# Attention, Fourier mixing and a feed-forward block in one kernel: the queries cut into seven tiles of 64 instead of four tiles of 64 and four of 49

## The chip, the cores and the metric

One Trainium2 chip, one of its cores. The time is the device time of one execution in microseconds (us). The kernel before took 907.45 us in the median of three runs (907.34 to 907.94). The profiled execution took 908.43 us, of which 906.0 us lie between its first and last instruction (its span), and 2.4 us around them.

## The reference

```python
def _attn_ref(q, k, v, cap):                      # q, k, v: 4 x 12 x 448 x 64, float32
    scores = (1 / np.sqrt(64)) * np.matmul(q, k.transpose(0, 1, 3, 2))
    scores = cap * np.tanh(scores / cap)
    scores = scores - np.max(scores, axis=-1, keepdims=True)
    attn = np.exp(scores)
    attn = attn / (np.sum(attn, axis=-1, keepdims=True) + 1e-09)
    return np.matmul(attn, v)

def _moe_ref(x, w_ch1, w_ch2):                    # x: 4 x 448 x 768, the 12 heads side by side
    mixed = np.real(np.fft.fft(np.fft.fft(x, axis=1), axis=2))
    u = x + mixed
    un = (u - mean(u)) / np.sqrt(var(u) + 1e-06)  # over the 768 features
    ch = np.maximum(un @ w_ch1, 0.0) @ w_ch2      # 768 x 3072, 3072 x 768
    return u + ch
```

## The kernel before, in words

Four batches; in each, twelve heads are worked on as six pairs, so 24 pairs follow each other. Keys lie on the partitions. `scores` (line 410) multiplies 64 keys of each of two heads (or 128 of one) with all queries: four products of 64 x 64 weights side by side in the four quarters of TensorE's array, 450 columns each, into one of two PSUM tiles `s`. ScalarE makes `tanh` (line 420) and `exp` (line 423) of each tile of 900 columns into one of five tiles `a`. `weigh` (line 439) takes 64 queries of `a` as weights and streams the values `vt` through them: 64 value columns and one column of ones, from which the denominators come. One pair of heads has seven units of `weigh`; six have 128 keys of one head, the seventh (the first unit of odd pairs, the last of even ones) has 64 keys of both. All of a pair adds up in one PSUM tile `av`, of which there is only one.

The queries are reordered into four groups of 112, 113, 112 and 113 rows (`ROWS`; the queries 0 and 224 stand twice, 450 in all), so that the four groups lie over each other: group 2 holds the mirror images of group 0, group 3 those of group 1, and the Fourier transform over the sequence begins with sums and differences of groups (`fold_tokens`). `weigh` cuts each group into 64 and 49 queries (where a group has 112, the last is the next group's first): four times two products for a unit of one head, the two of a pair side by side in the two column halves of the array, with the same values streamed through both.

When a pair is complete, VectorE adds the guard to the denominators (line 454), takes their reciprocals (455) and multiplies the whole tile with them into `u` (461, one instruction of 512 columns on 113 partitions). Only then is `av` free for the first product of the next pair. When the six pairs of a batch are there, VectorE folds them (480 to 500), TensorE makes two Fourier stages (`yps`, line 516; `pq`, line 544), VectorE combines and adds (536, 564, 568), takes moments and standardises, TensorE transposes (`pt`, line 628), and VectorE and ScalarE split the result into a high and a low part (`xs`). This work of a batch runs while the pairs of the next batch are in attention. VectorE also splits the weights of the feed-forward block into high and low parts (lines 675 to 709).

The feed-forward block is 3,450 products of 128 x 448 (`ph`, line 762; `po`, lines 797 and 820), twelve groups of four batches. The first group is interleaved with the last batch's Fourier work.

All instructions stand in one written plan: a table `ORDER` gives each step a number, the plan is sorted by it, and every engine executes its instructions in this order. DMAs are issued by SyncE in the same order, apart from the first load of queries.

Of the kernel before, what the change touches and what calls it, by code (L numbers as in the profile page):

```python
# [34 lines left out]
KODD, KEVEN = list(range(1, H2 // 2, 2)), list(range(0, H2 // 2 + 1, 2))  # L35
# [7 lines left out]
CNT = [len(r) for r in ROWS]  # L43
OFF = [sum(CNT[:g]) for g in range(4)]
R = max(CNT)

NT2 = CNT[0] + CNT[1] + 1

PERM = ROWS[0] + ROWS[1] + ROWS[2] + ROWS[3][2:]
OUT = [sum(CNT[:g]) for g in range(4)]  # L50

# [5 lines left out]
NK = len(KODD + KEVEN)  # L57
# [44 lines left out]
        265, 256, 308, 286, 489, 482, 521, 495, 721, 724, 710, 712, 839, 840, 844, 846  # L102
    ],
    "combine": [
        230, 249, 234, 245, 431, 437, 450, 453, 663, 673, 655, 684, 830, 832, 831, 833
    ],
    "denominators": [
        44, 74, 103, 125, 155, 178, 205, 246, 282, 317, 343, 372, 417, 464, 500, 537, 561, 596, 649,
        678, 715, 750, 776, 801
    ],  # L110
    "exp": [
# [19 lines left out]
    "load_constant": [
        214, 212, 237, 22
    ],
    "load_k": [
        0, 4, 6, 40, 43, 113, 134, 147, 186, 195, 257, 264, 344, 306, 389, 433, 456, 516, 519, 570, 583,
        672, 707, 719
    ],
    "load_q": [
        1, 12, 3, 34, 20, 61, 99, 108, 101, 144, 143, 169, 207, 232, 220, 262, 295, 302, 321, 342, 363,
        392, 427, 425, 462, 504, 492, 528, 543, 572, 619, 646, 657, 727, 726, 737  # L140
    ],
    "load_v": [
# [39 lines left out]
    "rows_copy": [
        362, 574, 794, 874
    ],
    "rows_out": [
        381, 444, 505, 466, 606, 622, 623, 615, 802, 814, 871, 824, 875, 900, 887, 877
    ],
    "scales": [
        2
    ],  # L190
    "scores": [
# [5 lines left out]
    ],  # L197
    "stage1": [
        224, 236, 226, 241, 419, 424, 438, 448, 647, 664, 644, 677, 827, 826, 829, 821
    ],  # L200
    "stage2": [
        260, 253, 293, 273, 469, 468, 490, 485, 717, 718, 691, 701, 837, 838, 843, 845
    ],
    "standardise": [
        348, 365, 357, 364, 575, 564, 550, 592, 780, 792, 782, 783, 883, 881, 867, 876
    ],
    "tanh": [
# [5 lines left out]
    ],  # L213
    "u_cols": [
        371, 374, 384, 391, 404, 407, 593, 594, 604, 607, 634, 636, 797, 798, 811, 812, 853, 860, 884,
        885, 889, 890, 892, 897
    ],
    "u_copy": [
        373, 376, 388, 395, 408, 420, 597, 599, 616, 618, 635, 642, 800, 805, 816, 823, 855, 865, 886,
        888, 893, 896, 898, 899  # L220
    ],
    "warmup": [
        8
    ],
    "weigh": [
# [54 lines left out]
def attention_fft_ffn(  # L280
# [60 lines left out]


    vt = new([P, 2, NC, D + 1], F32, "vt", 1, "vt")
    nc.gpsimd.memset(vt[:, :, :, D:], 1.0)

    qk = {}

# [109 lines left out]
    def normalise(p):  # L457
# [5 lines left out]
            pa[..., :D],  # L463
            den.to_broadcast([R, 4, 2, D]),
            op=mul,
        )

# [581 lines left out]
```

## Time and profile before

| | us |
|---|---|
| median of three runs | 907.45 |
| the profiled execution | 908.43 |
| its span | 906.0 |
| PE busy (TensorE's products) | 896.0 |
| DVE busy (VectorE) | 713.5 |
| ACT busy (ScalarE) | 326.6 |
| POOL busy (GpSimd) | 6.8 |

The granted TensorE clock is 1.00 of full speed throughout. PE counts products, whose ends are modelled, so 99% busy does not mean that it could do nothing more. ScalarE is busy 70% and more only in the first eight of 40 slices, which is the attention; VectorE is at 80% or more in most slices from the fourth on. Three stretches are of use: from 0 to 55 us the first batch is in attention alone; from 55 to 192.6 us the other pairs are in attention beside the Fourier work of the batches before; from 192.6 to about 268.5 us the last batch's Fourier work goes on beside the first products; after that the feed-forward block runs alone.

### The profile page before, as it was taken

To read this page: it belongs to the slowest core of one execution; us is meant where nothing else is said; L and a number is where in the kernel's file an instruction comes from. 1 tells how busy PE (TensorE), PEld (TensorE's weight loads), DVE (VectorE), ACT (ScalarE), POOL (GpSimd) and SP (SyncE) were. 2 spreads that over 40 slices of the span, in tenths; PEclk is the share of its full clock that TensorE was granted. 3 is DMA by queue.
4 is the path that set the end of the run, shared out by engine and by line. 5 is a ranking of instruction groups with operands and counts; after the bars stand their busy time and mean duration, and the time that the engine had idled before them with its cause. 6 is when DMAs were issued, how large, how long until landed. Compare 5 with 4: busy or idle time off the path is not lost.

```text
span 906.0 us, 18642 instructions
## 1 busy us (share of the span) xinstructions
PE 896.0 (99%) x7836; PEld 791.7 (87%) x7836; DVE 713.5 (79%) x1444; ACT 326.6 (36%) x503; POOL 6.8 (1%) x15
## 2 busy tenths in 40 slices
PE   9999999999899999999999999999999999999998
PEld 5667777788889999999999999999999999999998
DVE  3578889989998788888878788787787877878633
ACT  7988999962412222122122221212222122122200
POOL 0000000000000000000000000000000000000000
PEclk9999999999999999999999999999999999999999
DMA  6545444300202221211222111112211112121033
GB/s 203 163 141 137 112 119 129 108 8 1 91 18 74 60 71 52 63 53 53 68 60 68 54 52 53 53 54 66 57 53 54 53 53 57 57 62 53 18 122 122
DMA packets 50467, 66.64 MB, mean 74 GB/s; under 512 B 25424, under 2 KB 36560, under 8 KB 50384
## 3 DMA queue, kind: packets, MB, share of 16 engines
q1 hardware_dynamic: 50096, 65.13, 24.9%
q8 instruction: 61, 1.00, 0.4%
q10 hardware_dynamic: 288, 0.33, 0.1%
q14 instruction: 22, 0.18, 0.1%
HBM read 59.93 MB, written 5.52 MB: 72 GB/s over the span
## 4 chain that ended last, share of the span: by engine, by line
PE 94%; DVE 3%; ACT 1%; issue 0%; DMA 0%; SPq 0%; POOL 0%; DVEq 0%; POOLq 0%
PE ph L762 37%; PE po L797 37%; PE av L439 8%; PE s L410 7%; PE pq L544 2%; PE yps L516 1%; PE pt L628 1%; DMA vt<-vr 0%; PE warm L351 0%; DVE xs L329 0%; DVE xc L752 0%; DVE y L536 0%; ACT a L420 0%; DVE xc L829 0%; DVE hh L774 0%
## 5 line engine op out<-in xcount | busy, mean ns | idle before, releaser
L762 PE MATMUL ph<-xs,w 128*128 128x448 f32 x1728 | 352.8, 362 | 0.0
L797 PE MATMUL po<-hh,w 128*128 128x448 f32 (+1 forms) x1686 | 343.5, 362 | 3.2 <-DVE xc L829 3.2
L762 PEld LDWEIGHTS ph<-xs,w 128*128 128x128 f32 x1728 | 323.6, 187 | 21.8
L797 PEld LDWEIGHTS po<-hh,w 128*128 128x128 f32 x1686 | 314.4, 188 | 26.4 <-DVE xc L829 4.4
L805 DVE TENSOR_TENSOR xc<-xc,po 128x448 f32<-128x448 f32 (+1 forms) x281 | 172.3, 617 | 41.1 <-PE po L797 40.8
L675 ACT ACTIVATE wt<-raw 128x384 f32<-128x384 f32 x84 | 46.7, 555 | 229.0 <-DVE w L709 229.0
L774 DVE SCALAR_TENSOR_TENSOR hh<-ph,hh 128x448 fp32r<-128x448 f32 x96 | 60.0, 625 | 86.4 <-ACT hh L773 85.7
L773 ACT ACTIVATE hh<-ph 128x448 fp32r<-128x448 f32 x96 | 52.4, 545 | 177.3 <-PE ph L762 177.3
L439 PEld LDWEIGHTS av<-vt,a 128*49 128x49 f32 (+3 forms) x3072 | 85.3, 130 | 23.6 <-issue 12.6
L439 PE MATMUL av<-vt,a 128*49 128x65 f32 (+3 forms) x3072 | 91.2, 222 | 1.4 <-issue 0.9
L420 ACT ACTIVATE a<-s,tscale 128x900 f32<-128x900 f32 x84 | 82.7, 1017 | 10.2 <-PE s L410 9.9
L324 ACT CAST w<-wt 128x384 fp32r<-128x384 f32 x84 | 42.8, 510 | 119.1 <-DVE wt L684 119.1
L423 ACT ACTIVATE a<-a,capt 128x900 f32<-128x900 f32 x84 | 84.8, 1051 | 0.5
L410 PE MATMUL s<-q,k 64*64 64x450 f32 x672 | 75.7, 555 | 0.5 <-ACT a L420 0.4
L684 DVE SCALAR_TENSOR_TENSOR wt<-wt 128x384 f32<-128x384 f32 x96 | 53.6, 558 | 9.2
L681 DVE SCALAR_TENSOR_TENSOR wt<-raw,wt 128x384 uint32<-128x384 uint32 x96 | 53.6, 559 | 3.3
L709 DVE TENSOR_TENSOR w<-wt 128x384 fp32r<-128x384 f32 x96 | 53.6, 558 | 3.3
L703 DVE SCALAR_TENSOR_TENSOR wt<-raw,wt 128x384 f32<-128x384 uint32 x96 | 53.5, 558 | 2.9
L329 DVE TENSOR_TENSOR wt<-wt,w 128x384 f32<-128x384 f32 x96 | 52.8, 550 | 0.0
L410 PEld LDWEIGHTS s<-q,k 64*64 64x64 f32 x672 | 21.4, 134 | 23.0 <-issue 10.3
L678 DVE TENSOR_SCALAR wt<-raw 128x384 uint32<-128x384 uint32 x96 | 34.2, 357 | 1.1
L700 DVE TENSOR_SCALAR wt<-wt 128x384 uint32<-128x384 uint32 x96 | 34.0, 354 | 0.5
(63 smaller groups left out, 345.2 us busy)
## 6 DMA issues: line engine op xcount, KB each, us to landing
raw<-w2r SPq DMA_DIRECT2D x48, 384.0 KB
raw<-w1r SPq DMA_DIRECT2D x48, 384.0 KB
q<-qr SPq DMA_DIRECT2D x35, 225.5 KB
outT<-xc SPq DMA_DIRECT2D x23, 224.0 KB
k<-kr SPq DMA_DIRECT2D x12, 256.0 KB
vt<-vr SPq DMA_DIRECT2D x24, 128.0 KB
k<-kr SPq DMA_DIRECT2D x12, 192.0 KB
vt<-vr SPq DMA_DIRECT2D x24, 96.0 KB
```

Of the source, the lines that this page charges most:

```text
L410: nc.tensor.matmul(ps_t[t][h * D : (h + 1) * D, n, :SQ], kt[q, k][rows, k0, h], qk[q, x][rows, :SQ], start=True, stop=True,)
L420: nc.scalar.activation(a_t[t], ps_t.pop(t)[:, :, :SQ], AF.Tanh, scale=tscale)
L423: nc.scalar.activation(a_t[t], a_t[t], AF.Exp, scale=capt)
L439: nc.tensor.matmul(pa_t[p][q0:q1, j, g * (D + 1) : (g + 1) * (D + 1)], a_t[t][rows, n, OFF[g] + q0 : OFF[g] + q1], vt[rows, p % 2, i], sta ...
L681: nc.vector.scalar_tensor_tensor(tu, hi.bitcast(U32), 0xC0000000, tu, op0=ALU.bitwise_and, op1=ALU.bitwise_or)
L684: nc.vector.scalar_tensor_tensor(t, w, HI_MIN, t, op0=ALU.is_ge, op1=mul)
L703: nc.vector.scalar_tensor_tensor(w, lo, 2.0**-52, w, op0=mul, op1=mul)
L709: nc.vector.tensor_tensor(ws[c][1][:, sl], t, w, op=add)
L762: nc.tensor.matmul(ph[:, :S], w_[:, dc * P : (dc + 1) * P], x_, start=(k_ == 0), stop=(k_ == 3 * NDC - 1),)
L774: nc.vector.scalar_tensor_tensor(hh[:, 1], ph[:, :S], 0.0, f32(hh[:, 0]), op0=ALU.max, op1=sub)
L797: nc.tensor.matmul(po[:, q0:q1], w_[:, dc * P : (dc + 1) * P], hh[:, x_, q0:q1], start=(k_ == 0), stop=(k_ == 3 * GF - 1),)
L805: nc.vector.tensor_tensor(ac[:, q0:q1], ac[:, q0:q1], po[:, q0:q1], op=add)
```

## The change

The queries 0 and 224 no longer stand twice: 448 queries, seven tiles of 64. The rows now lie in four groups of 128, 128, 96 and 96. The first 96 of groups 0 and 1 have their mirror images in groups 2 and 3; the last 32 of groups 0 and 1 are queries of which both mirror halves are kept unfolded.

In `weigh`, a unit of one head has six products (three times two column halves) instead of eight. The seventh tile of a head is issued together with that of the other head of the pair: one goes to the lower column half, the other to the upper, in the unit of the second head, each with its own values streamed through. For the unit of both heads it is twelve products and then the two seventh tiles, one in a lower and one in an upper quarter. So a pair has 56 products instead of 64. The ones now stand in front of the values, and two products of a pair write 66 columns instead of 65.

`normalise` has five VectorE instructions instead of one: a product of 128 columns on 32 partitions, a memset of two columns, two products of 64 columns on 64 partitions, and one of 384 columns on 128. GpSimd sets a part of `u` to zero once per batch. `stage1` has 128 and 129 columns instead of 113 and reads 128 partitions; `combine` works on 256 columns instead of 226. `fold_tokens` to `standardise` work on 128 partitions instead of 113 with as many columns as before. `ORDER` has new numbers throughout; of its lines two are shown.

```diff
-ODD = [k for m in KODD for k in (m, H2 - m)]
-EVEN = [k for m in KEVEN for k in (m, H2 - m)][:-1]
-ROWS = [ODD, EVEN, [S - k for k in ODD], [(S - k) % S for k in EVEN]]
-QUERIES = [k for r in ROWS for k in r]
+FOLD = 96
+KS = [ks[: FOLD // 2] for ks in (KODD, KEVEN)]
+KS[0] += [k for m in KODD[FOLD // 2 :] for k in (m, S - m)]
+KS[1] += [0] + [k for m in KEVEN[FOLD // 2 :] for k in (m, S - m)] + [H2 // 2]
+ROWS = [[k for m in ks for k in (m, (H2 - m) % S)] for ks in KS]
+ROWS[1][-1] = S - H2 // 2
+ROWS += [[S - k for k in r[:FOLD]] for r in ROWS]
+QUERIES = ROWS[0] + ROWS[1] + ROWS[2] + ROWS[3][D:] + ROWS[3][:D]
...
     "load_k": [
-        0, 4, 6, 40, 43, 113, 134, 147, 186, 195, 257, 264, 344, 306, 389, 433, 456, 516, 519, 570, 583,
+        0, 28, 50, 37, 91, 106, 128, 161, 177, 245, 258, 264, 315, 376, 372, 438, 494, 477, 515, 581,
...
     def weigh(u):
-        for g in range(4):
+        def tile(j, g, half, rows, n, i):
+            q = (2 * g + half) * D if g < 3 else 6 * D
+            w = D + 1 + int(g == 2 and c == 0 and half != j)
+            nc.tensor.matmul(
+                pa_t[p][half * D : (half + 1) * D, j, g * (D + 1) : g * (D + 1) + w],
+                a_t[t][rows, n, q : q + D],
+                vt[rows, p % 2].rearrange("k n c -> k (n c)")[:, i * (D + 1) : i * (D + 1) + w],
...
+        for g in range(3):
             for j in (0, 1) if head is None else (head,):
                 rows = slice(P) if head is not None else slice(j * D, (j + 1) * D)
-                for q0, q1 in ((0, D), (D, R)):
-                    nc.tensor.matmul(
-                        pa_t[p][q0:q1, j, g * (D + 1) : (g + 1) * (D + 1)],
-                        a_t[t][rows, n, OFF[g] + q0 : OFF[g] + q1],
-                        vt[rows, p % 2, i],
...
+                for half in range(2):
+                    tile(j, g, half, rows, n, i)
+        for j in range(2):
+            if head is None:
+                tile(j, 3, j, slice(j * D, (j + 1) * D), n, i)
+            elif head == 1:
+                tile(j, 3, j, slice(P), n - 1 + j, i - 1 + j)
...
     def denominators(p):
         if b not in u_t:
             u_t[b] = new([P, 4, DM], F32, f"x{b % 2}", 1, "u")
+            nc.gpsimd.memset(u_t[b][FOLD:, 3], 0.0)
...
     def normalise(p):
-        nc.vector.tensor_tensor(
-            u_t[b][:R, :, c0 : c0 + 2 * D].rearrange("q g (j c) -> q g j c", j=2),
-            pa[..., :D],
-            den.to_broadcast([R, 4, 2, D]),
-            op=mul,
-        )
+        def part(out, rows, j, g):
+            x = pa[rows, j, g]
+            nc.vector.tensor_tensor(out, x, den[rows, j, g].to_broadcast(x.shape), op=mul)
+
+        part(u[D:FOLD, :, 3], slice(FOLD, P), slice(2), 2)
+        nc.vector.memset(den[FOLD:, :, 2], 0.0)
+        for j in range(2):
+            part(u[:D, j, 3], slice(j * D, (j + 1) * D), j, 3)
+        part(u[:, :, :3], slice(P), slice(2), slice(3))
...
     def stage1(b, p, sd):
-                        ps[q0:q1, o : o + NK],
-                        f[: CNT[c], 2 * n + c, p0 + q0 : p0 + q1],
-                        seqT[n][: CNT[c], c],
+                        ps[q0:q1, o0:o1],
+                        f[:, 2 * n + c, p0 + q0 : p0 + q1],
+                        seqT[n][:, c, : o1 - o0],
```

TensorE at the fifth change of pair, before: the last products of one pair (`av`), the scores of two key tiles (`s`, eight products), and the first products of the next pair.

```order
328 L439 MATMUL av<-vt,a 64x65
329 L439 MATMUL av<-vt,a 49x65
330 L439 MATMUL av<-vt,a 64x65
331 L439 MATMUL av<-vt,a 49x65
332 L410 MATMUL s<-q,k 64x450 x8
333 L439 MATMUL av<-vt,a 64x65
334 L439 MATMUL av<-vt,a 49x65
335 L439 MATMUL av<-vt,a 64x65
336 L439 MATMUL av<-vt,a 49x65
```

The same place now:

```order
40 L439 MATMUL av<-vt,a 64x65 x3
41 L410 MATMUL s<-q,k 64x448 x8
42 L439 MATMUL av<-vt,a 64x65 x42
43 L410 MATMUL s<-q,k 64x448 x8
44 L439 MATMUL av<-vt,a 64x65 x14
```

Between the two pairs stand eight products of scores, as before; the products around them all have 64 queries.

TensorE at the sixteenth change of pair, before:

```order
1207 L439 MATMUL av<-vt,a 64x65
1208 L439 MATMUL av<-vt,a 49x65
1209 L439 MATMUL av<-vt,a 64x65
1210 L439 MATMUL av<-vt,a 49x65
1211 L410 MATMUL s<-q,k 64x450 x8
1212 L439 MATMUL av<-vt,a 64x65
1213 L439 MATMUL av<-vt,a 49x65
1214 L439 MATMUL av<-vt,a 64x65
1215 L439 MATMUL av<-vt,a 49x65
```

And now:

```order
221 L439 MATMUL av<-vt,a 64x66
222 L439 MATMUL av<-vt,a 64x65 x4
223 L439 MATMUL av<-vt,a 64x66
224 L439 MATMUL av<-vt,a 64x65 x31
225 L410 MATMUL s<-q,k 64x448 x12
226 L439 MATMUL av<-vt,a 64x65 x5
227 L439 MATMUL av<-vt,a 64x66
228 L439 MATMUL av<-vt,a 64x65 x4
```

Here the scores of three key tiles stand between the pairs instead of two.

VectorE at the end of a pair in the middle of a weight conversion (`wt`, `w`), before (the second pair):

```order
24 L700 TENSOR_SCALAR wt<-wt 128x384
25 L326 CAST w_294<-wt 128x384
26 L703 SCALAR_TENSOR_TENSOR wt<-raw,wt 128x384
27 L454 TENSOR_SCALAR den<-av,guard 113x8
28 L455 RECIPROCAL den<-den 113x8
29 L461 TENSOR_TENSOR u<-av,den 113x4x128
30 L329 TENSOR_TENSOR wt<-wt,w_294 128x384
```

And now (the first pair):

```order
19 L697 SCALAR_TENSOR_TENSOR wt<-raw,wt 128x384
20 L700 SCALAR_TENSOR_TENSOR wt<-wt 128x384
21 L466 TENSOR_SCALAR den<-av,guard 128x8
22 L467 RECIPROCAL den<-den 128x8
23 L477 TENSOR_TENSOR u<-av,den 32x128
24 L480 MEMSET den 32x2
25 L477 TENSOR_TENSOR u<-av,den 64x64 x2
26 L477 TENSOR_TENSOR u<-av,den 128x2x3x64
27 L716 TENSOR_SCALAR wt<-wt 128x384
```

Five instructions stand between the reciprocals and the next conversion step where one stood.

## Rows read from the trace of the kernel before

**Rows 1.** Busy time of each engine by stretch: us, PE, PEld, DVE, ACT, POOL, PEclk, DMA, GB/s.

```profile
0.00:15.00 15.00, 13.20 (x179) 7.97 (x182) 2.68 (x11) 10.13 (x13) 0.75 (x7) 1.00 0.75 230
15.00:55.00 40.00, 39.67 (x966) 26.69 (x960) 26.25 (x61) 39.54 (x43) 0.00 (x0) 1.00 0.56 154
55.00:192.60 137.60, 136.14 (x3075) 98.34 (x3065) 121.75 (x281) 123.84 (x151) 4.36 (x6) 1.00 0.42 114
192.60:268.50 75.90, 72.53 (x467) 64.81 (x467) 70.19 (x143) 22.91 (x44) 1.67 (x2) 1.00 0.09 29
268.50:906.00 637.50, 634.48 (x3176) 593.86 (x3174) 492.60 (x950) 130.16 (x253) 0.00 (x0) 1.00 0.21 61
```

**Rows 2.** The page's chain that ended last, shares of the span by engine.

```profile
PE 94%; DVE 3%; ACT 1%; issue 0%; DMA 0%; SPq 0%; POOL 0%; DVEq 0%; POOLq 0%
```

**Rows 3.** Timeline at the fifth change of pair: start, duration, instruction, idle before.

```profile
42.25 1.70 PE L410 MATMUL s<-q,k 64*64 64x450 f32 x16
...
42.52 0.23 DVE L454 TENSOR_SCALAR den<-av,guard 113x8 f32<-113x8 f32 x1 [4.67 <-PE av L439]
...
42.78 0.20 DVE L455 RECIPROCAL den<-den 113x8 f32<-113x8 f32 x1
...
43.02 0.69 DVE L461 TENSOR_TENSOR u<-av,den 113x512 f32<-113x512 f32 x1
...
43.63 0.35 DVE L677 TENSOR_SCALAR wt<-raw 128x384 uint32<-128x384 uint32 x1
43.78 0.58 PEld L439 LDWEIGHTS av<-vt,a 64*64 64x64 f32 x32 [0.60 <-PE s L410]
...
43.89 0.35 DVE L678 TENSOR_SCALAR wt<-raw 128x384 uint32<-128x384 uint32 x1
```

**Rows 4.** Timeline at the sixth change of pair.

```profile
49.05 0.69 DVE L461 TENSOR_TENSOR u<-av,den 113x512 f32<-113x512 f32 x1
...
50.10 0.31 PEld L439 LDWEIGHTS av<-vt,a 128*64 128x64 f32 x8 [0.71 <-ACT a L423]
```

**Rows 5.** Timeline, TensorE's weight loads in two unbroken runs of `weigh`.

```profile
46.42 1.94 PEld L439 LDWEIGHTS av<-vt,a 128*64 128x64 f32 x64 [0.71 <-ACT a L423]
...
85.87 2.88 PEld L439 LDWEIGHTS av<-vt,a 128*64 128x64 f32 x96 [0.71 <-PE s L410]
```

**Rows 6.** The chain in order of time: start, duration, engine, line, count.

```profile
22.30 1.67 PE s L410 x16
...
40.30 0.92 PE s L410 x8
...
63.14 1.56 PE yps L516 x32
```

**Rows 7.** VectorE's groups by shape: count | busy us, mean ns | idle before.

```profile
L568 DVE TENSOR_TENSOR u<-u,pq 113x384 f32<-113x384 f32 x32 | 15.5, 546 | 0.5 <-PE pq L544 0.5
L329 DVE TENSOR_TENSOR xs<-xc,xs 128x448 fp32r<-128x448 f32 x24 | 14.3, 616 | 0.0
L752 DVE TENSOR_TENSOR xc<-xc,mean 128x896 f32<-128x896 f32 x12 | 13.0, 1085 | 0.0
...
L536 DVE TENSOR_TENSOR y<-yps,yh 97x226 f32<-97x226 f32 x32 | 12.3, 394 | 5.5 <-ACT yh L324 4.9
...
L603 DVE COPY rowt<-rt 8x113 f32<-8x113 f32 x4 | 1.0, 257 | 0.0
...
L574 DVE MEMSET stat<- 128x8 f32 x4 | 0.3, 65 | 0.0
```

**Rows 8.** Waits from 55 to 192 us: who, for whom, us in total, times, longest.

```profile
DVE den L454 <- PE av L439: 5.4, 10, 1.1
...
DVE y L536 <- ACT yh L324: 4.4, 4, 1.9
...
DVE u L564 <- PE pq L544: 1.6, 3, 0.8
```

**Rows 9.** Waits from 192.6 to 268.5 us.

```profile
PEld po L797 <- DVE xc L829: 4.4, 3, 1.9
```

More of the change, by code (lines that the diff above doesn't have):

```diff
@@ L34 @@
 H2 = S // 2
-KODD, KEVEN = list(range(1, H2 // 2, 2)), list(range(0, H2 // 2 + 1, 2))
-ODD = [k for m in KODD for k in (m, H2 - m)]
-EVEN = [k for m in KEVEN for k in (m, H2 - m)][:-1]
-ROWS = [ODD, EVEN, [S - k for k in ODD], [(S - k) % S for k in EVEN]]
-QUERIES = [k for r in ROWS for k in r]
+FOLD = 96
+KODD, KEVEN = (list(range(1, H2 // 2, 2)), list(range(2, H2 // 2, 2)))
+KS = [ks[: FOLD // 2] for ks in (KODD, KEVEN)]
[4 more added lines that the diff above has]
+ROWS += [[S - k for k in r[:FOLD]] for r in ROWS]
+CNT = [len(r) for r in ROWS]
+OUT = [sum(CNT[:g]) for g in range(4)]
+PERM = [k for r in ROWS for k in r]
+QUERIES = ROWS[0] + ROWS[1] + ROWS[2] + ROWS[3][D:] + ROWS[3][:D]
 SQ = len(QUERIES)
@@ L42 @@
 KT = (0, 4, 7)
[L43 to L50, printed above, removed]
+NT2 = CNT[0] + CNT[1]
 NJE, NJO = DM // 4 + 2, DM // 4
@@ L184 @@
     ],
     "rows_out": [
-        381, 444, 505, 466, 606, 622, 623, 615, 802, 814, 871, 824, 875, 900, 887, 877
+        405, 418, 466, 416, 621, 661, 657, 675, 810, 861, 840, 851, 888, 922, 928, 939
     ],
     "scales": [
-        2
-    ],
-    "scores": [
[5 rows of a table removed]
[L197 to L206, printed above, removed]
@@ L207 @@
-    "tanh": [
[5 rows of a table removed]
[L213 to L224, printed above, removed]
-    "weigh": [
[9 rows of a table removed]
+        4
+    ],
+    "scores": [
[5 rows of a table added]
+    ],
+    "stage1": [
+        233, 242, 236, 246, 434, 435, 443, 446, 640, 658, 651, 664, 827, 829, 824, 821
+    ],
@@ new lines @@
+    "stage2": [
+        259, 254, 269, 291, 473, 472, 505, 511, 709, 716, 684, 687, 838, 845, 839, 849
+    ],
+    "standardise": [
+        363, 354, 347, 368, 567, 576, 583, 580, 790, 789, 791, 786, 876, 879, 883, 874
+    ],
+    "tanh": [
[5 rows of a table added]
+    ],
+    "u_cols": [
+        374, 375, 391, 392, 409, 414, 599, 597, 616, 620, 628, 633, 796, 802, 814, 808, 862, 869, 884,
+        889, 891, 896, 892, 899
+    ],
+    "u_copy": [
+        385, 390, 401, 412, 424, 428, 610, 614, 622, 625, 631, 636, 801, 807, 817, 819, 865, 873, 885,
+        890, 895, 898, 904, 905
+    ],
@@ L263, in _dft_constants @@
             feat[n, :FW, p, NJO : NJO + len(j)] = np.where(d == FW - 1, 0.5, 1.0) * f(2 * np.pi * ((d * j) % DM) / DM)
-    ks = np.array(KODD + KEVEN)
-    seq = np.zeros((2, P, 2, NK), np.float64)
-    for n, f in enumerate((np.cos, np.sin)):
-        for c in range(2):
-            t = np.array(ROWS[c])[:, None]
-            self_ = np.where(t % (S // 2) == 0, (0.5, 0.0)[n], 1.0) * (1, -1)[n * c]
-            seq[n, : CNT[c], c] = self_ * f(2 * np.pi * ((t * ks[None, :]) % S) / S)
+    ks = np.array(KS[0] + KS[1])
+    seq = np.zeros((2, P, 2, NK + 1), np.float64)
+    for c in range(2):
+        t = np.array(ROWS[c])[:, None]
+        seq[0, :, c, :NK] = np.cos(2 * np.pi * ((t * ks) % S) / S)
+        seq[1, :, c, 1 - c : 1 - c + NK] = (1, -1)[c] * np.sin(2 * np.pi * ((t * ks) % S) / S)
+    seq[1, :, 0, 0] = -seq[1, :, 0, NK]
+    seq[0, :, 0, NK - 1] = seq[1, :, 0, NK] = 0
     return feat.astype(np.float32), seq.astype(np.float32)
@@ L343, in attention_fft_ffn @@
     vt = new([P, 2, NC, D + 1], F32, "vt", 1, "vt")
-    nc.gpsimd.memset(vt[:, :, :, D:], 1.0)
+    nc.gpsimd.memset(vt[:, :, :, :1], 1.0)
     qk = {}
@@ L535, in combine @@
             out = bass.AP(y.tensor, y.offset + k_, [list(y.ap[0]), [step, 2], [2, NK]])
-            nc.vector.tensor_tensor(out, ps[:, :, 0], half, op=op)
+            nc.vector.tensor_tensor(out, ps[:, 0::3], half, op=op)
     def stage2(b, n, par):
@@ L563, in add_u @@
             for u_, f in ((u_lo, lo), (u_hi, hi)):
-                nc.vector.tensor_tensor(u_, u_, f[:, None].to_broadcast([R, 2, m, 2]), op=add)
+                nc.vector.tensor_tensor(u_, u_, f[:, None].to_broadcast([P, 2, m, 2]), op=add)
             return
@@ L597, in rows_cols @@
         nc.tensor.matmul(
-            ps[:8, :R], stat[b][:R].rearrange("q g a -> q (g a)"), ident[:R, :R], start=True, stop=True
+            ps[:8, :P], stat[b].rearrange("q g a -> q (g a)"), ident, start=True, stop=True
         )
     def rows_copy(b):
-        r = rowt[b] = new([8, R], F32, "rowt", 1, "rowt")
-        nc.vector.tensor_copy(r, d_t.pop(("r", b))[:8, :R])
+        r = rowt[b] = new([8, P], F32, "rowt", 1, "rowt")
+        nc.vector.tensor_copy(r, d_t.pop(("r", b))[:8, :P])
     def rows_out(b, g):
-        off, skip = OUT[g], (0, 0, 0, 2)[g]
-        cnt = CNT[g] - skip
+        off, cnt = OUT[g], CNT[g]
         if b not in lnrow:
@@ L625, in u_cols @@
         pt = d_t["u", b, p] = bank(b, p % 2, "pt")
-        for g in (3, 0, 1, 2):
-            off, cnt = OUT[g] - (0, 0, 0, 2)[g], CNT[g]
+        for g in range(4):
+            off, cnt = OUT[g], CNT[g]
             nc.tensor.transpose(
```

117 lines of the change are left out of this document (60 added, 57 removed), and 60 rows, old and new, of the table ORDER.

## The prediction

> **What bounds the kernel now.** I read the table by stretch first, then the chain, then the timeline at the changes of pair, then the waits. By stretch [rows 1], the granted clock is 1.00 (2.4 GHz) everywhere, so no term below comes from the clock. From 268.5 us to the end TensorE runs the feed-forward block with VectorE at 492.6 of 637.5 us; the change touches nothing there, so whatever is gained or lost must be gained or lost before 268.5 us. Before it no engine is alone. TensorE is on 94% of the chain [rows 2], but from 15 to 55 us ScalarE is busy 39.54 of 40.00 us, from 55 to 192.6 us VectorE is busy 121.75 and ScalarE 123.84 of 137.6 us, and from 192.6 to 268.5 us VectorE is busy 70.19 of 75.9 us. What one engine saves counts only as far as the other two have room.
>
> The place to look at is the change of pair, because there is one `av` tile. At the fifth [rows 3] the scores start at 42.25 us, VectorE's first instruction at 42.52, the reciprocal at 42.78, the product at 43.02 for 0.69 us; it ends at 43.71, and the next `weigh` loads at 43.78. So this change is held by VectorE to the last 0.07 us. At the sixth [rows 4] the product ends at 49.74 and `weigh` starts at 50.10: 0.36 us, of which 0.29 are slack. The two kinds alternate (a pair that ends with the unit of both heads, and one that begins with it).
>
> **TensorE's savings.** A run of 64 loads of `weigh` takes 1.94 us and one of 96 takes 2.88 us [rows 5]: 0.94 us for 16 more slots (two column halves side by side), 59 ns a slot. Each pair had 28 slots and has 25 (six units of one head: 24, now 21; the unit of both heads keeps four, in quarters), each in two passes: 24 x 3 x 2 = 144 slots, 8.5 us. The product of 49 queries was no cheaper than its neighbour of 64, so nothing is lost there. Scores: 0.75 us for eight records (16 take 1.67, 8 take 0.92 [rows 6]), 84 such tiles, 448 for 450 columns: 0.3 us. Against it `stage1`: 32 records are 16 slots of 113 columns in 1.56 us [rows 6], 98 ns; 15 more columns are 13 ns, and for 128 slots that is 1.7 us. Scores stand in four more runs than before in the attention; a run costs 0.17 us beyond its work (0.92 less 0.75) and about as much where `weigh` resumes: 1.2 us. Net TensorE: -8.5 - 0.3 + 1.7 + 1.2 = -5.9 us, if nothing waits.
>
> **VectorE's cost.** One product of 0.69 us [rows 3] becomes five instructions. None of their forms is in the trace. A 113-wide copy out of PSUM takes 257 ns, 226 columns take 394 and 384 take 546, a memset 65 [rows 7]. I take 275 for 128 columns, 240 for 64, 546 for 384: 0.275 + 0.065 + 2 x 0.24 + 0.546 = 1.37 us. An instruction that needs its predecessor starts 0.03 us after its end (42.52 + 0.23, then 42.78 [rows 3]): four more hand-offs, 0.12. Upper bound 1.49 us, +0.80 a pair. Two neighbours that don't need each other overlap by 0.09 us (43.63, 0.35 long, then 43.89 [rows 3]); if three of the hand-offs do that, 0.36 less, 1.13 us, +0.44. A gain is excluded, since 640 columns in five instructions replace 512 in one. I take +0.80: the memset follows a reader of what it clears, the last product reads what the memset cleared, and the nearest row for such short steps is the pair 454 to 455.
>
> The Trainium skill ("VectorE: DVE Perf Modes", section "Two Vector instructions with no wait between them") says that an instruction whose input or output starts in another group of 32 partitions than the last one's is held until every earlier vector instruction has finished. The overlapping pair in [rows 3] both start at partition 0, and no run here shows a change of group; the new pieces start at 96, 64 or 0 in turn. By the rule the step is the upper bound, by the overlapping row the lower.
>
> Other VectorE work: `combine` has 30 columns more, 30 ns on 394 [rows 7], 32 times, 1.0 us. Folds, moments and standardising keep their columns. ScalarE loses four of 900 columns, 0.4%, 0.7 us in all. GpSimd's four memsets lie on an engine that is busy 4.36 of 137.6 us [rows 1]; what they write is first read by the folds, six pairs later.
>
> **DMA order.** At the start 96 KB of values and 384 KB of raw weights stand ahead of the second load of queries; at 230 GB/s [rows 1] that is 2.1 us. The fourth score tile is the first that needs it, and this waits for ScalarE to free a PSUM tile; I cost it at nothing, at most 2 us.
>
> **The sum by stretch.** *To 55 us* (changes 1 to 6, all with eight scores between). A change of the held kind costs 0.80, of the other 0.80 - 0.29 = 0.51, 0.66 on average; TensorE saves 6 x 59 ns = 0.35 a pair. 0.3 x 6 = 1.8 us lost if TensorE sets the pace, none if ScalarE does, since a stall there replaces time that TensorE would have waited for `exp`. I take +0.9.
>
> *55 to 192.6 us* (18 pairs). TensorE: -18 x 0.35 = -6.3, scores -0.2, `stage1` of three batches +1.3, more runs +1.2. Thirteen of its changes of pair have cover: Fourier products, or twelve scores (2.25 us) instead of eight, as at the sixteenth. The seventh, tenth, eleventh and twenty-third have eight scores or fewer and pay 0.80, 0.51, 0.80, 0.80 = 2.9. TensorE comes to -1.1. VectorE: +18 x 0.80 = 14.4, +0.8 for `combine`; the new order puts six conversion steps and two folds earlier, before 55 us, where VectorE is idle 13.75 us [rows 1]: -3.9. Net +11.3 us. Its idle time that such work can use is what it spends waiting for `av`, 5.4 us; the waits for ScalarE's copy and for `pq` (4.4 and 1.6 [rows 8]) come from a chain of dependences and go only in part. So VectorE is 11.3 - 5.4 = 5.9 us over, less what of those 6.0 can go. I take +1.5 for the stretch, with -1 and +5 as ends.
>
> *192.6 to 268.5 us*. TensorE waits there for VectorE's `xc` [rows 9], so VectorE's list counts whole: from the last normalise to the last of the additions at line 829, the new order has two `xc` products more (1.085 each), two `xs` fewer (0.616 each), and 0.03 x 8: +1.2 us [rows 7].
>
> Total 0.9 + 1.5 + 1.2 = 3.6 us on a span of 906.0: 909.6, and with the 2.4 us around it 912.0 for the profiled execution. This stood 1.0 above the median of the runs, so I forecast 911.0 us. A measurement of this kernel can tell a change over 0.2% (1.8 us) from none: below 905.6 is faster, above 909.3 slower.
>
> **Rivals.**
> *The pieces overlap, and the savings cancel the costs.* +0.44 a pair: to 55 us 0.44 - 0.15 = 0.30 on average, under the 0.35 saved, 0. To 192.6 us VectorE is +18 x 0.44 + 0.8 - 3.9 = 4.8 over, under the 5.4 of waits for `av`; TensorE is -6.3 - 0.2 + 1.3 + 1.2 + 1.5 = -2.5. With the tail's +1.2: -1.3, or 906.2 us. For it: the overlap at 43.63; against it: the dependences listed above.
>
> *TensorE's saving comes through.* The order has been made for the longer step, the changes of pair that matter have twelve scores, and VectorE's added work goes into its idle time. Then -5.9, of which 6 x 0.35 = 2.1 is lost before 55 us to ScalarE: -3.8, 903.7 us. For it: 13.75 us of idle VectorE before 55 us and [rows 4]'s slack; against it: VectorE's 70.19 of 75.9 us in the last stretch, which this leaves no longer.
>
> *The seventh tiles don't run side by side.* Their column halves stream different values. If they take turns, the three slots saved a pair are given back: 8.5 us on top of the forecast's, about 919 us. Against it: one score tile in seven has halves that stream different queries, the run at 22.30 us has such a tile in it, and it takes 1.67 us, 0.17 + 2 x 0.75 like any [rows 6].
>
> **How the numbers follow.** Forecast (step serial, VectorE short) 0.46, own range 909 to 914; overlap 0.30, 904.5 to 908.5; saving comes through 0.20, 901 to 906; taking turns 0.04. Slower is most of the first (0.38), the last (0.04) and a little of the second (0.02): 0.44. Faster is most of the third (0.17), 0.08 of the second and 0.01 of the first: 0.26. Within 0.2% is the rest, 0.30. The range that leaves out two in ten reaches from the middle of the third case to the upper end of TensorE's and VectorE's bounds in the first: 904.0 to 915.5.
>
> **What the profile after would show.** `weigh` at 59 ns a slot with 21 + 4 slots a pair, and the two seventh tiles starting within some 10 ns of each other. From the denominators' start to the end of normalise 2.0 us where it was 1.19; `weigh` then starting 0.07 us later at changes 1, 3, 5 and 7. VectorE over 95% busy from 55 to 192.6 us, with its waits for `av` gone, and the last stretch about a microsecond longer. I am wrong if normalise ends within 1.65 us of its start, if VectorE still waits for `av` 5 us in the second stretch, or if the feed-forward block, taken alone, changes.

## The result, and the profile after

The changed kernel takes 913.27 us (median of 7 runs, 910.39 to 914.49), the kernel before 907.46 (907.28 to 909.07). The ratio is 1.0054, 95% interval 1.004 to 1.0068: slower by 0.5%. The forecast was 911.0 us.

| profiled execution, us | before | after |
|---|---|---|
| its time | 908.43 | 913.63 |
| its span | 906.0 | 910.8 |
| PE busy | 896.0 | 892.0 |
| DVE busy | 713.5 | 728.4 |

Two stretches of the kernel after, with the columns of [rows 1]:

```profile
15.00:55.00 40.00, 35.67 (x778) 22.76 (x774) 24.19 (x73) 37.59 (x42) 0.00 (x0) 1.00 0.55 150
55.00:192.60 137.60, 132.81 (x2804) 93.56 (x2804) 130.01 (x342) 125.94 (x154) 6.22 (x8) 1.00 0.40 110
```

The clock is again 1.00. From 15 to 55 us TensorE and ScalarE are both less busy than before (35.67 for 39.67, 37.59 for 39.54): something else holds them. From 55 to 192.6 us VectorE has gone from 121.75 to 130.01 us of 137.6. In the chain that ended last VectorE has grown from 3% to 7% [rows 2]:

```profile
PE 90%; DVE 7%; issue 1%; ACT 1%; POOL 0%; DVEq 0%; POOLq 0%
```

The fifth change of pair after, for [rows 3] (timeline):

```profile
45.69 0.23 DVE L466 TENSOR_SCALAR den<-av,guard 128x8 f32<-128x8 f32 x1 [4.45 <-PE av L439]
...
46.19 0.30 DVE L477 TENSOR_TENSOR u<-av,den 32x128 f32<-32x128 f32 x1
...
46.55 0.06 DVE L480 MEMSET den<- 32x2 f32 x1
...
46.64 1.05 DVE L477 TENSOR_TENSOR u<-av,den 64x64 f32<-64x64 f32 x3
...
47.76 0.54 PEld L439 LDWEIGHTS av<-vt,a 64*64 64x64 f32 x27 [1.38 <-PE s L410]
47.79 0.59 PE L439 MATMUL av<-vt,a 64*64 64x65 f32 x25 [0.63 <-PE s L410]
```

From 45.69 to 47.69 it is 2.00 us, and `weigh` loads 0.07 us later, as at this change before. TensorE has stood idle for 0.63 us when `weigh` begins. It does so at each of the first six changes, for 0.48 to 1.14 us, 4.0 us together; in the kernel before it stands idle for less than 0.1 us at all of them. The three last products take 1.05 us together. Their durations, in VectorE's groups by shape (for [rows 7]), add up to 1.00, so they stand one behind the other with gaps, and none overlaps:

```profile
L477 DVE TENSOR_TENSOR u<-av,den 128x384 f32<-128x384 f32 x24 | 13.4, 558 | 0.8
...
L477 DVE TENSOR_TENSOR u<-av,den 64x64 f32<-64x64 f32 x48 | 10.6, 221 | 1.1
L477 DVE TENSOR_TENSOR u<-av,den 32x128 f32<-32x128 f32 x24 | 7.1, 296 | 0.7
```

On TensorE the chain in order of time (for [rows 5] and [rows 6]) shows unbroken runs of `weigh`:

```profile
27.24 1.85 PE av L439 x56
...
39.84 1.04 PE av L439 x28
...
64.38 1.75 PE yps L533 x32
```

28 records more (14 products, each recorded twice) are 14 slots and take 0.81 us, 58 ns a slot: the halves run side by side, the seventh tiles' too. `stage1` takes 1.75 us; 1.56 and 16 x 13 ns were forecast, 1.77.

To see where the time went, the stretches are cut at events: the first, seventh and last denominators' start. Before (the same columns):

```profile
15.43:54.40 38.97, 38.64 (x932) 25.98 (x928) 25.72 (x59) 38.94 (x43) 0.00 (x0) 1.00 0.56 154
54.40:192.71 138.31, 136.85 (x3079) 98.83 (x3072) 122.29 (x283) 124.01 (x152) 4.36 (x6) 1.00 0.42 115
192.71:906.00 713.29, 706.91 (x3640) 658.56 (x3640) 562.79 (x1092) 153.08 (x297) 1.67 (x2) 1.00 0.20 58
```

After:

```profile
16.52:60.27 43.75, 38.98 (x852) 25.23 (x848) 29.15 (x81) 39.79 (x44) 0.00 (x0) 1.00 0.58 156
60.27:196.08 135.81, 131.31 (x2789) 92.92 (x2790) 128.31 (x342) 123.85 (x151) 6.22 (x8) 1.00 0.38 103
196.08:910.80 714.72, 708.07 (x3642) 658.58 (x3640) 564.45 (x1097) 152.99 (x297) 1.27 (x2) 1.00 0.19 58
```

The first denominators start 1.1 us later, the first six changes of pair lose 4.8 us, the middle gains 2.5, the rest loses 1.4. Other executions of the same instructions agree on the middle (135.8 us in the control below, 135.7 in the run on the start) and the rest (714.7 in both), but not on the first six changes: 44.3 us in the control, 42.5 in the run on the start. In the middle VectorE does 6.0 us more and is idle 8.5 us less (16.02, now 7.50). The waits there that are left, 55 to 192 us, for [rows 8]:

```profile
DVE den L466 <- PE av L439: 0.9, 4, 0.4
DVE y L553 <- ACT yh L324: 0.9, 1, 0.9
```

### The profile page after: what moved, and what is told of

It is laid out like the page before. It is cut to its first block, busy times and chain, and to the rows that moved or that the text cites. A ratio compares the mean times of both kernels' runs of the same rounds, so it can differ in the third digit from the quotient of the medians.

```text
span 910.8 us, 17992 instructions
## 1 busy us (share of the span) xinstructions
PE 892.0 (98%) x7452; PEld 784.8 (86%) x7452; DVE 728.4 (80%) x1540; ACT 327.1 (36%) x503; POOL 9.7 (1%) x19
## 4 chain that ended last, share of the span: by engine, by line
PE 90%; DVE 7%; issue 1%; ACT 1%; POOL 0%; DVEq 0%; POOLq 0%
PE po L813 37%; PE ph L778 37%; PE av L439 7%; PE s L410 6%; PE pq L561 2%; DVE u L477 1%; PE yps L533 1%; DVE xc L768 1%; DVE tf L502 1%; DVE tf L496 1%; DVE ff L515 0%; DVE y L553 0%; PE warm L351 0%; DVE xs L329 0%; PE pt L644 0%
## 5 line engine op out<-in xcount | busy, mean ns | idle before, releaser
L439 PEld LDWEIGHTS av<-vt,a 128*64 128x64 f32 (+1 forms) x2688 | 76.7, 137 | 33.7 <-issue 17.2
L439 PE MATMUL av<-vt,a 128*64 128x65 f32 (+1 forms) x2688 | 82.5, 223 | 8.0 <-issue 3.7
L420 ACT ACTIVATE a<-s,tscale 128x896 f32<-128x896 f32 x84 | 82.5, 1005 | 11.8 <-PE s L410 9.7
L423 ACT ACTIVATE a<-a,capt 128x896 f32<-128x896 f32 x84 | 83.6, 1039 | 0.4
L410 PE MATMUL s<-q,k 64*64 64x448 f32 x672 | 78.5, 560 | 1.5 <-ACT a L420 1.5
```

The source lines that it names most:

```text
L410: nc.tensor.matmul(ps_t[t][h * D : (h + 1) * D, n, :SQ], kt[q, k][rows, k0, h], qk[q, x][rows, :SQ], start=True, stop=True,)
L420: nc.scalar.activation(a_t[t], ps_t.pop(t)[:, :, :SQ], AF.Tanh, scale=tscale)
L423: nc.scalar.activation(a_t[t], a_t[t], AF.Exp, scale=capt)
L439: nc.tensor.matmul(pa_t[p][half * D : (half + 1) * D, j, g * (D + 1) : g * (D + 1) + w], a_t[t][rows, n, q : q + D], vt[rows, p % 2].rearr ...
```

## The experiments

All ratios are to the kernel before, timed beside each run on the same chip.

| run | time, us | ratio | 95% interval | step, us |
|---|---|---|---|---|
| control (changed kernel) | 912.04 | 1.0038 | 1.0025 to 1.0052 | 1.99 |
| start | 911.39 | 1.0034 | 1.0022 to 1.0047 | 1.99 |
| one product | 902.65 | 0.9938 | 0.9926 to 0.9951 | 1.05 |
| before, five pieces | 921.12 | 1.0144 | 1.013 to 1.0158 | 1.99 |
| same partitions | 906.34 | 0.9975 | 0.9965 to 0.9985 | 1.63 |
| memset on GpSimd | 909.53 | 1.0015 | 1.0005 to 1.0025 | 1.74 |
| old order | 916.22 | 1.0089 | 1.0073 to 1.0104 | 1.99 |
| before, new order | 908.14 | 1.0002 | 0.999 to 1.0014 | 1.19 |
| moves on GpSimd | 906.49 | 0.9989 | 0.9978 to 0.9999 | 1.43 |
| moves, every second pair | 907.22 | 0.9991 | 0.9982 to 1.0 | 1.44 and 1.73 |

The step is the time from the denominators' start to the end of normalise's last product at changes of pair with nothing between.

**Control.** 

> The changed kernel unaltered, as a control on the same chip as the three beside it. Every theory expects the ratio that it had, 1.0054 (1.004 to 1.0068), so about 912.4 us beside 907.5 for the kernel before, and normalise ending 1.99 us after the denominators' start at the early changes of pair.

 Measured: ratio 1.0038, 912.04 us (910.5 to 913.91). Its first ACT tile comes earlier than in the profile above, though the mask comes as late (next run).

**The start.** After the change GpSimd's first memset of `u` stands in front of the mask for the warm-up products, and these start at 2.20 us instead of 1.35. In the profile after, the first `tanh` was 0.8 us late too (7.33 for 6.56).

```diff
-            u_t[b] = new([P, 4, DM], F32, f"x{b % 2}", 1, "u")
-            nc.gpsimd.memset(u_t[b][FOLD:, 3], 0.0)
+            for b_ in (0, 1) if b == 0 else (b,):
+                u_t[b_] = new([P, 4, DM], F32, f"x{b_ % 2}", 1, "u")
+                (nc.vector if b == 0 else nc.gpsimd).memset(u_t[b_][FOLD:, 3], 0.0)
```

> The changed kernel with the first two memsets of u taken from GpSimd's queue, where they stand in front of the mask that TensorE's first products need, and given to VectorE just before the first denominators. Theory (GpSimd's queue delays the start, and the delay reaches the end): the first tanh starts at about 6.6 us instead of 7.33, and the whole is 0.8 us shorter than the changed kernel (912.4 instead of 913.3). Rival (ScalarE or VectorE absorbs the delay later): the first tanh is as early, the end the same within 0.3 us.

 Timeline of the control, then of this run:

```profile
2.20 3.35 PE L351 MATMUL warm<-ident 128*128 128x128 f32 x14 [2.20 <-POOL ident masks.py:199]
...
5.48 1.85 PE L410 MATMUL s<-q,k 64*64 64x448 f32 x16
...
6.04 0.14 PEld L410 LDWEIGHTS s<-q,k 64*64 64x64 f32 x4 [0.25 <-issue]
6.41 0.14 PEld L410 LDWEIGHTS s<-q,k 64*64 64x64 f32 x4 [0.23 <-issue]
6.66 1.01 ACT L420 ACTIVATE a<-s,tscale 128x896 f32<-128x896 f32 x1 [0.98 <-PE s L410]
```

```profile
1.35 3.35 PE L351 MATMUL warm<-ident 128*128 128x128 f32 x14 [1.35 <-POOL ident masks.py:199]
...
4.78 3.88 PE L410 MATMUL s<-q,k 64*64 64x448 f32 x24
...
5.55 0.28 PEld L410 LDWEIGHTS s<-q,k 64*64 64x64 f32 x4 [0.47 <-issue]
...
6.30 0.28 PEld L410 LDWEIGHTS s<-q,k 64*64 64x64 f32 x4 [0.47 <-issue]
...
6.61 1.01 ACT L420 ACTIVATE a<-s,tscale 128x896 f32<-128x896 f32 x1 [1.13 <-PE s L410]
```

The late mask does hold the scores: they start at 5.48 us in the control and 5.49 in the profile after, but at 4.78 here. The control's first `tanh` comes at 6.66 all the same, because its half tiles of scores follow each other faster: 0.37 us from 6.04 to 6.41, where this run takes 0.75 (5.55 to 6.30) and the profile after 0.75 too, with its `tanh` at 7.33. The trace's first record of the granted clock begins at 5.77 us in the control, ahead of its faster half tile, and at 7.27 here and 8.43 in the profile after, behind these slower ones. A lower clock ahead of that record would explain the two paces; no row shows what was granted there, and the tables' 1.00 does not tell. The two executions that ran at the same pace differ by 0.7 us, as the theory had it. Whether it reaches the end is not decided: 912.04 and 911.39 have overlapping intervals.

**One product.**

```diff
...
-        part(u[D:FOLD, :, 3], slice(FOLD, P), slice(2), 2)
-        nc.vector.memset(den[FOLD:, :, 2], 0.0)
-        for j in range(2):
-            part(u[:D, j, 3], slice(j * D, (j + 1) * D), j, 3)
         part(u[:, :, :3], slice(P), slice(2), slice(3))
```

> The changed kernel with only the product of 384 columns left of normalise's five instructions: the rows of the seventh tiles and the unfolded rows are not normalised (they are zero or as they came). VectorE's step falls by about 0.93 us a pair, to some 1.06 us from the denominators' start to the end, below the 1.19 of the kernel before; TensorE has all it has in the changed kernel. Theory (the step on VectorE is what turned a saving of TensorE into a loss): 901 to 905 us, 8 to 12 below the changed kernel. Rival (TensorE's saving is worth nothing here, or the new order itself costs): 907 us or more.

 Measured 902.65, inside the theory's 901 to 905: with a step of 1.05 us the kernel is 5.4 us below the one before. TensorE's saving comes through, though not all of the 5.4 need be its own, since the step is also 0.14 us shorter than before. VectorE in the middle is short of work again (waits, 55 to 192 us):

```profile
DVE den L466 <- PE av L439: 7.3, 11, 1.5
```

**The kernel before with five pieces.** Its product of 512 columns (line 461 of the kernel before) becomes

```diff
...
+        part(u[D : R - 32, :, 3], slice(96, R), slice(2), 2)
+        nc.vector.memset(den[96:R, :, 2], 0.0)
+        part(u[:D, 0, 3], slice(D), 0, 3)
+        part(u[: R - D, 1, 3], slice(D, R), 1, 3)
+        part(u[:R, :, :3], slice(R), slice(2), slice(3))
```

> The kernel before with its one product of 512 columns cut into five instructions of the same shapes and starting partitions as in the changed kernel (which rows they write is wrong, their number and sizes are what counts), and with a part of u set to zero once per batch; TensorE's products and the order stay as before. The step becomes 1.99 instead of 1.19 us. Theory (the step costs 0.80 us where TensorE waits for the change of pair, and VectorE runs out of room from 55 to 192.6 us): 913 to 920 us, of which about 4 us before 55 us. Rival (most of it lies beside other work in any case, and the loss of the changed kernel comes from its new order): at most 909.5 us.

 The pieces have the columns and starting partitions of the changed kernel, but lie on 17, 64, 49 and 113 partitions; the step is the same 1.99 us. Measured 921.12, 13.0 us over the kernel before and more than expected. Its stretches by event, and two of its waits from 55 to 192 us:

```profile
15.71:60.10 44.39, 39.24 (x932) 26.16 (x928) 29.70 (x83) 39.83 (x43) 0.00 (x0) 1.00 0.54 149
60.10:206.43 146.33, 139.08 (x3079) 98.57 (x3072) 133.13 (x352) 124.20 (x151) 5.82 (x8) 1.00 0.38 105
```

```profile
ACT a L420 <- PE s L410: 13.8, 14, 2.4
...
DVE den L456 <- PE av L439: 5.8, 8, 1.6
```

Six changes of pair with 0.80 us more each lose 5.4 us. Of this 1.3 us is a stop inside a run of `weigh` at 58.35 us, for which no releaser is shown; the rest is 0.69 each. The other seventeen lose 8.0 us, 0.47 each. The rival is excluded. That VectorE runs out of room there is not what happened: it waits 5.8 us for `av`, as long as before (5.4), while ScalarE's waits for scores rise from 9.1 to 13.8 us.

**Same partitions.** Why do neighbours that don't need each other not overlap?

```diff
...
-        part(u[D:FOLD, :, 3], slice(FOLD, P), slice(2), 2)
-        nc.vector.memset(den[FOLD:, :, 2], 0.0)
+        part(u[: FOLD - D, :, 3], slice(P - FOLD), slice(2), 2)
+        nc.vector.memset(den[: P - FOLD, :, 2], 0.0)
         for j in range(2):
-            part(u[:D, j, 3], slice(j * D, (j + 1) * D), j, 3)
+            part(u[:D, j, 3], slice(D), 0, 3)
```

> The changed kernel with the five instructions of normalise all reading and writing from partition 0 on (sizes, number, order and the dependence through the memset as they are; so which rows are normalised is wrong). Theory (the two products of 64 columns and the last one start late because their first partition differs from the one before): they now start some 80 to 90 ns before the end of the one before, three times some 0.1 us; normalise ends 1.65 to 1.75 us after the denominators' start instead of 1.99, and at the 0.42 us per us of step that leaving out the pieces showed (9.4 us for 24 x 0.94) the whole is 2.5 to 3.5 us below the changed kernel, about 909. Rival (they wait for the memset and for results, whatever the partitions): 1.90 us or more, and 912.

 VectorE at the fifth change of pair (timeline), and what its four products took (line 477 alone: shortest, median, longest in ns):

```profile
44.49 0.23 DVE L466 TENSOR_SCALAR den<-av,guard 128x8 f32<-128x8 f32 x1 [5.00 <-PE av L439]
...
44.99 0.53 DVE L477 TENSOR_TENSOR u<-av,den 32x128 f32<-32x128 f32 x2
45.32 0.06 DVE L480 MEMSET den<- 32x2 f32 x1
45.44 0.67 DVE L477 TENSOR_TENSOR u<-av,den 64x64 f32<-64x64 f32 x2
46.04 0.67 DVE L496 TENSOR_TENSOR tf<-u 128x512 f32<-128x512 f32 x1
```

```profile
L477 DVE TENSOR_TENSOR u<-av,den x4: 206/244/541, 45.0 to 45.6; 64x64 f32<-64x64 f32 x2, 32x128 f32<-32x128 f32 x1, 128x384 f32<-128x384 f32 x1
```

The same five instructions end 1.62 us after the start, not 2.00. The second product of 64 columns starts at 45.44, before the first ends (44.99 + 0.53 = 45.52); the last two, 0.21 and 0.54 long, take 0.67 together. The dependence through the memset is still there, so it is the starting partition that keeps the pieces apart in the changed kernel. The Trainium skill's rule ("VectorE: DVE Perf Modes", section "Two Vector instructions with no wait between them") holds here in both directions. The edit also makes both products of 64 columns read the first head, but the next run, which reads what the changed kernel reads, shows the same: there the 384 columns start 0.08 us before the end of the 64 from the same partition, and the pieces from partitions 64 and 96 start 0.01 to 0.03 us after the end of the one before. The time fell by 5.7 us from the control, twice what was expected.

**The memset on GpSimd** (with the start of the second run).

```diff
...
-        part(u[D:FOLD, :, 3], slice(FOLD, P), slice(2), 2)
-        nc.vector.memset(den[FOLD:, :, 2], 0.0)
-        for j in range(2):
-            part(u[:D, j, 3], slice(j * D, (j + 1) * D), j, 3)
+        part(u[:D, 0, 3], slice(D), 0, 3)
         part(u[:, :, :3], slice(P), slice(2), slice(3))
+        part(u[:D, 1, 3], slice(D, P), 1, 3)
+        part(u[D:FOLD, :, 3], slice(FOLD, P), slice(2), 2)
+        nc.gpsimd.memset(u[FOLD:, :, 2], 0.0)
```

> The changed kernel with the start as in the run before (first memsets of u on VectorE), normalise in the order 64 columns at partition 0, 384 columns at partition 0, 64 columns from partition 64, 128 columns from partition 96, and the memset of the denominators replaced by one of u on GpSimd behind them; it computes the same. Theory: one instruction less on VectorE and one hold less, normalise's last piece ends 1.75 us after the denominators' start instead of 1.99, 24 x 0.24 x 0.42 = 2.4 us less than the changed kernel, about 909.5. Rival (the folds that read u now wait for GpSimd, or GpSimd's writes slow VectorE): no gain, 912 or more.

 Measured 909.53, as the theory had it.

**Old order, and new order alone.** The table `ORDER` of one kernel in the other:

```diff
     "load_k": [
-        0, 28, 50, 37, 91, 106, 128, 161, 177, 245, 258, 264, 315, 376, 372, 438, 494, 477, 515, 581,
+        0, 4, 6, 40, 43, 113, 134, 147, 186, 195, 257, 264, 344, 306, 389, 433, 456, 516, 519, 570, 583,
...
```

> The changed kernel with the table ORDER of the kernel before, so that only the seven tiles and the five pieces are new. Theory (the step costs what its cover leaves open, and the new order gives it cover): 5.9 us of TensorE's work less than the kernel before with five pieces (921.1), 915 to 918, so 3 to 6 us above the changed kernel. Rival (the new order is what made the changed kernel slower than the one before): 907 to 910.

> The kernel before with the table ORDER of the changed kernel: four tiles of 64 and four of 49, one product in normalise. Theory (the order helps, if only with the longer step): 904 to 907.5 us, no more than the kernel before. Rival (the new order costs time by itself, with its two products of xc more in the last part of the Fourier work): 909 or more.

 The first came out at 916.22, as the theory had it, 4.9 us under the kernel before with five pieces: that is the seven tiles, with the longer `stage1` and `combine` that come with them. The second came out at 1.0002, between the two: by itself the new order neither gains nor costs. Its stretches by event and its wait for `av`, from 55 to 192 us:

```profile
15.34:55.52 40.18, 40.18 (x948) 26.28 (x944) 25.25 (x57) 39.43 (x44) 0.00 (x0) 1.00 0.63 173
55.52:192.25 136.73, 134.85 (x3062) 97.01 (x3058) 116.22 (x274) 123.74 (x151) 4.76 (x6) 1.00 0.38 102
```

```profile
DVE den L454 <- PE av L439: 10.6, 12, 1.8
```

It lengthens the first six changes by 1.2 us, with two tiles of scores more in front of the seventh denominators. It takes 6.1 us of VectorE's work out of the middle (122.29, now 116.22), and VectorE waits 10.6 us there for `av`. With the five pieces the new order is worth 4.2 us (916.22 to 912.04); without them it is worth nothing. That it is this room which is used fits the place of the gain (the middle takes 142.92 us in the old order and 135.81 in the new), but is argued, not tried alone.

**The moves on GpSimd,** a version to beat both (again with that start):

```diff
...
+        part(u[D:, 1, 3], slice(D, P), 1, 3)
         part(u[:, :, :3], slice(P), slice(2), slice(3))
+        part(u[:D, 0, 3], slice(D), 0, 3)
+        nc.gpsimd.tensor_copy(u[:D, 1, 3], u[D:, 1, 3])
+        nc.gpsimd.tensor_copy(u[D:FOLD, :, 3], u[FOLD:, :, 2])
+        nc.gpsimd.memset(u[FOLD:, :, 2:], 0.0)
```

> The run with the memset on GpSimd taken further; it computes the same. VectorE makes three products: 64 columns from partition 64 to partition 64, then 384 and 64 columns at partition 0; GpSimd then copies the second head's seventh tile and the unfolded rows to their partitions inside u and clears what is left behind. Theory (only the time until av is free counts, and holds are paid where the first partition changes): the last product ends 1.40 us after the denominators' start (1.75 in that run, 1.99 in the changed kernel), 0.35 x 24 x 0.42 = 3.5 us less, about 906. Rival (every second pair is followed at once by folds that read u; they now wait some 1 to 1.5 us for GpSimd, and from 55 us on VectorE has no room): 908 or more.

 Timeline at the sixth change of pair, and the folds' wait in the first 270 us:

```profile
48.44 0.94 DVE L478 TENSOR_TENSOR u<-av,den 64x64 f32<-64x64 f32 x3
...
48.73 0.23 POOL L483 COPY u<-u 64x64 f32<-64x64 f32 x1 [3.43 <-DVE u L478]
49.38 0.29 POOL L484 COPY u<-u 32x128 f32<-32x128 f32 x1 [0.42 <-DVE u L478]
49.73 0.31 POOL L485 MEMSET u<- 32x256 f32 x1
50.07 1.29 DVE L498 TENSOR_TENSOR tf<-u 128x512 f32<-128x512 f32 x2 [0.70 <-POOL u L485]
```

```profile
DVE tf L498 <- POOL u L485: 3.2, 5, 0.7
```

The step ends at 49.38, 1.44 us after 47.94. The folds wait 0.7 us behind it, but only five times. At 906.49 us, near the theory's 906, it is below both kernels, 0.11% under the one before (0.01 to 0.22%).

**The same for every second pair,** so that no fold waits:

```diff
...
+        if p % 2 == 0:
             part(u[D:, 1, 3], slice(D, P), 1, 3)
+        else:
+            part(u[D:FOLD, :, 3], slice(FOLD, P), slice(2), 2)
+            part(u[:D, 1, 3], slice(D, P), 1, 3)
...
+        if p % 2 == 0:
             nc.gpsimd.tensor_copy(u[:D, 1, 3], u[D:, 1, 3])
...
```

> The same for the first, third and fifth pair of a batch only; after the others the folds follow at once, and there VectorE makes four products (128 columns from partition 96, 64 from partition 64, then 384 and 64 at partition 0), of which the last ends about 1.72 us after the denominators' start. It computes the same. Theory: half of the gain of the run beside it, and no wait of the folds: 907.5 to 908. Rival (the folds' wait is what counts): below the run beside it, 906 or less.

 Measured 907.22, between the theory (907.5 to 908) and the rival (906 or less); the intervals of the two overlap almost wholly, so whether the folds' wait or the longer step costs more stays open.

## Why the prediction was right, and where its steps were wrong

The direction, the time and the main mechanism hold: the longer step of VectorE costs more than TensorE saves. Two terms of the sum were mis-sized, in opposite directions, so that the total came out near the forecast is in part luck.

**VectorE's step: right.** 1.49 us from the reciprocal to the end was taken as the upper bound, and 46.19 to 47.69 is 1.50. The rival in which the pieces overlap fell, and for the reason that the Trainium skill's rule gave: on the same partitions they overlap. The time is then 906.3, near that rival's 906.2, but the parts are not the rival's: the six changes lose 3.6 us (42.53) where it had none, and the middle gains 6.2 (132.08) where it had 2.5.

**TensorE's saving: right by the slot.** 144 slots at 58 ns are 8.4 us, 8.5 were forecast, and the seventh tiles do not take turns; they start 20 or 38 ns apart like all neighbours of such a run, not some 10. Less of it reaches the end: 5.9 us net were forecast, 7.1 without the four more runs of the new order, and with the same pieces and the old order the seven tiles save 4.9 (921.12 to 916.22).

**To 55 us: wrong, too low.** +0.9 us was taken, at most 1.8. The six changes lost 4.8 in the profile after, 5.3 in the control and 3.5 in the run on the start; 1.2 of it comes with the new order (40.18 for 38.97), which the sum did not count here. The sentence that failed is "none if ScalarE does, since a stall there replaces time that TensorE would have waited for `exp`". A stall of `weigh` also delays the scores behind it, and then ScalarE waits for them. Its waits for scores between 15 and 60 us rose from

```profile
ACT a L420 <- PE s L410: 1.0, 2, 0.6
```

to

```profile
ACT a L420 <- PE s L410: 3.7, 3, 1.6
```

An engine busy 39.54 of 40.00 us has no room to make that good. That 4.8 is just six times 0.80 holds for one execution alone. TensorE's saving is not shown to be worth nothing there: with five pieces and the old order the seven tiles bring the six changes from 44.39 to 41.21 us, in one execution each, of which 1.3 is the stop without a releaser.

**55 to 192.6 us: wrong, the other way.** +1.5 was taken; by event it is -2.5, of which the new order alone gives -1.6 (136.73 for 138.31). VectorE's added work was put at 11.3 us and its busy time rose by 6.0: the new order takes 6.1 us out of this stretch, where 3.9 were counted, and the hand-offs between the pieces, counted as work, show as idle time. Of the waits for ScalarE's copy and `pq`, 6.0 us that "go only in part", 0.9 is left. VectorE is busy 130.01 of 137.6 us, 94.5%, where over 95% was announced, and its waits for `av` are 0.9 us.

**192.6 us to the end: the size right by luck, the cause wrong.** +1.2 was forecast from the order's list of `xc` and `xs`; +1.4 was measured. But the new order alone gives 713.6 us from the last denominators to the end of the span (905.9 less 192.25), +0.4; the five pieces alone give 713.3 (919.7 less 206.43), nothing. So +1.1 comes with the rest of the new code in the new order. With one product it is 714.2 (899.9 less 185.73), so about half of the 1.1 goes with the small pieces; which part makes the other half was not tried. The feed-forward block keeps its time, as forecast: from the 501st record of `po` to the end it takes 486.7 us before and 486.6 after.

**The start and the DMA order.** The DMA order was put at nothing, and up to the first denominators it cost nothing (15.35 and 15.59 us in the control and the run on the start, 15.43 before). Behind them, at about 17 us, TensorE waits for a load of keys: 0.9 us in the control, 0.2 in the run on the start, not in the profile after. The mask behind GpSimd's memset was overlooked: the prediction looked at what reads `u`, not at what waits behind it on GpSimd. It costs the scores' start 0.7 us; whether it costs the kernel any time stays open.

The rival "TensorE's saving comes through" (903.7) is near what one product gives, 902.65: its failing condition was the step. The five pieces cost the changed kernel 9.4 us (control less one product).

My factor of 0.42 us per us of step was too simple. From 1.05 to 1.63 us the time rises by 3.7, from 1.63 to 1.99 by 5.7. VectorE's waits for `av` in the middle are 7.3, 3.3 and 0.9 us at these steps. That more of each added piece reaches the end once they are used up is a reading of these three, not a test.

What stays open: executions of one kernel differ by up to 4 us (the changed one 910.39 to 914.49; the one before 907.28 to 909.07 beside it, and 906.81 to 910.53 beside the run with the same partitions). Part of it may lie in stops inside a run of `weigh` for which no releaser is shown: 0.88 us in the control, 1.28 with five pieces, 0.93 and 0.61 with the same partitions. In the run on the start the control's 84 records are unbroken. Timeline of TensorE, control and then that run:

```profile
48.76 1.97 PE L439 MATMUL av<-vt,a 128*64 128x65 f32 x60
51.61 0.92 PE L439 MATMUL av<-vt,a 128*64 128x65 f32 x24 [0.88 <-issue]
```

```profile
48.27 2.67 PE L439 MATMUL av<-vt,a 128*64 128x65 f32 x84
```

## What to carry to other kernels

Where one accumulator is freed by another engine, price a change by that engine's step from the last product to the release, at every hand-over: a saving forecast at 5.9 us on the engine that leads the chain was turned into a loss by 0.80 us there. Do not cost a stall at nothing because a third engine is saturated; ask whether it is fed through the stalled one. Cut a VectorE step so that neighbours start on the same partitions, and give what has to cross partitions to an engine with room.

## What the runs showed of the hardware

The price of a change of starting partition on VectorE: five instructions took 1.50 us from the first product's start to the last one's end, and 1.12 us (44.99 to 46.11) when all started at partition 0.

GpSimd's copy of 32x128 took 0.29 us while VectorE waited (49.38, above), but 1.93 us where it started beside two folds, at the fifth change of pair of the same run:

```profile
42.91 1.28 DVE L498 TENSOR_TENSOR tf<-u 128x512 f32<-128x512 f32 x2
43.00 1.93 POOL L484 COPY u<-u 32x128 f32<-32x128 f32 x1 [0.42 <-DVE u L478]
```

The Trainium skill ("SBUF — State Buffer", section "Who interferes with whom") says that a VectorE instruction with two inputs in SBUF contends with a GpSimd instruction that reads SBUF; the folds have two such inputs, and this agrees. But the folds end at 44.19 and the copy at 44.93, so they are not all of it: two steps of the weight conversion with one input each follow them, and where the copy started beside two such steps and no fold (31.27 us) it took 0.68.
